# Attention with block sums and a gated FFN on one core: the transpose of the block sums ahead of a unit's stores, their copies a step later, and one pair's neighbor keys three steps sooner

## The chip, the core and the metric

The kernel runs on one core of a Trainium2 chip. The core has five engines with a queue of instructions each: PE (TensorE, matrix products, with its weight loads shown apart as PEld), DVE (VectorE), ACT (ScalarE), POOL (GpSimd, here almost only the issuer of loads) and SP (SyncE, here only an issuer of stores and of transposing DMAs). Each queue runs in order. The metric is the device time of one execution in microseconds; the median of several runs counts.

## What is computed

Sparse attention for 4 batches, 8 heads, 768 tokens of width 64: every token sees its neighbors at a distance under 16 and, for each of the 24 blocks of 32 tokens, the maximum of the block's keys with the mean of the block's values. Then a gated feed-forward layer with a residual gate over the 3072 tokens.

```python
k_sum = k.reshape(B, H, nb, block, D).max(axis=3)
v_sum = v.reshape(B, H, nb, block, D).mean(axis=3)
scores_l = where(|i - j| < 16, scale * q @ k.T, -1e9)
scores_s = scale * q @ k_sum.T + log(block)
a = softmax(concat([scores_l, scores_s]))
x = a @ concat([v, v_sum])                      # heads side by side: 3072 x 512
ffn = (gelu(x @ w_gate) * (x @ w_val)) @ w_out  # 512 -> 1536 -> 512
out = x + sigmoid(x @ w_res) * ffn
```

## The kernel before

The work is cut into eight units (`u` 0 to 7), each one half of a batch: 384 tokens (`TU`). Batch is `b = u // 2`, `half = u % 2`, and the batch to be prepared next is `nb = b + 1`. The order of the instructions is written out by hand, and each engine runs its queue in that order; semaphores make an instruction wait for what it reads and for what it overwrites.

A unit begins with the twelve steps `fo` 0 to 11 of the FFN's first layer. Each step makes the products `g` and `vv` on PE (L398, four matmuls each), the Gelu `ge` on ACT (L404) and the product `gvT` on DVE (L405). `g` and `vv` lie in four PSUM accumulators (tag `mm`) that are used in turn. Between the steps, small pieces that prepare the next unit or batch are put in: `values_step(u, fo)` and the `if` lines of the loop. After the twelve steps comes the rest of the unit: the scores of the next unit (`s_step`, L330, then the exponential on ACT and the mask on DVE, L347), the residual gate (`res_step`, L416, L422), the second FFN layer (`ffn_step`, L432), the products with the values (`av_step`, L362, scaled on DVE at L370 and L372 into `xn`), the transposes of `xn` (`xt_step` on PE, L381, or `xt_dma` on SP, L386), and per 128 tokens `end_step`, which makes `o` on DVE (L437, L439) and stores it (L443). The stores go by SP's queue in units 0, 1, 2 and 7 and by POOL's in units 3 to 6.

The operands of the attention are prepared like this:

- `kW` (one tile per batch parity and pair of heads, pairs 0 to 3) holds for each 64-token tile its own keys, 16 neighbor keys on each side, and the 24 block maxima; `qT` holds the transposed queries. `turn_batch(b, p0, p1)` transposes keys and queries of pairs p0 to p1-1 from `k_sb` and `q_sb` by DMA on SP: per pair two for `kW` (L251) and one for `qT` (L254). For batch 1, pairs 2 and 3 are turned at the start of unit 1, pairs 0 and 1 by PE.
- `k_rest(kw)` then makes the block maxima (L209, L211) and copies the neighbor keys (L213, L214) and the maxima (L215). For batch 1 all of it is on DVE; for batches 2 and 3 the two neighbor copies are on ACT.
- `vext` holds the values; `v_spread` (L291, L294) copies them on DVE to the odd tiles. For batches 2 and 3 the block sums come in four pieces: `turn_values` transposes the values on SP (L261, in step 0 of units 2 and 4), `block_sums` sums them on DVE into `vsT` (L267, steps 8 to 11 of units 2 and 4), `turn_sums` transposes `vsT` into `vsB` by one DMA on SP (L271), and `vsum_bc` copies `vsB` into rows 96 to 127 of `vext` (L303), on ACT for the first half of the batch in units 3 and 5, on DVE for the second half in units 4 and 6.

In the kernel before, `turn_sums` is issued in step 0 of units 3 and 5, so on SP's queue it stands behind what the unit before it issued there. The three lines that matter for its place:

```python
if half == 1 and 1 < nb < B and fo == 0:
    turn_sums()
    turn_batch(nb, NP - 1, NP)
```

Of the kernel before, what the change touches and what calls it, by code (L numbers as in the profile page):

```python
# [15 lines left out]
def kernel(  # L16
# [11 lines left out]
    nc = tc.nc  # L28
    B, H, S, D = q.shape
# [8 lines left out]
    FO = DFF // 128  # L38
    QT = 64
    NT = S // QT  # L40
    HT = NT // 2
# [3 lines left out]
    NP = H // 2  # L45
# [27 lines left out]
    kW = [[const.tile([128, NT, 128], BF16, name=f"kW{i}_{p}") for p in range(NP)] for i in range(2)]  # L73
# [30 lines left out]
    with tc.manual_schedule():  # L104

        def vext_consts(i):
            nc.vector.memset(vext[i][:, :, :, D:D + 1], 1.0)
            nc.vector.memset(vext[i][0:WIN, 0], 0.0)
            nc.vector.memset(vext[i][64:96, NT - 1], 0.0)
            nc.vector.memset(vext[i][64:64 + WIN, NT - 1, :, D:D + 1], 1.0)  # L110
# [57 lines left out]
        def gate(t):  # L168
            nc.gpsimd.tensor_copy(tick[:], t)
# [36 lines left out]
        def k_rest(kw, copy=nc.vector.tensor_copy):  # L206
            own = kw[:, :, OWN:OWN + QT].rearrange("d t (n w) -> d t n w", w=BLK)
            km = work.tile([128, NT, 2, BLK // 2], BF16, tag="km", name="km")
            nc.vector.tensor_max(km[:], own[:, :, :, 0:BLK // 2], own[:, :, :, BLK // 2:BLK])  # L209
            ks = work.tile([128, NB], BF16, tag="ks", name="ks")  # L210
            nc.vector.tensor_reduce(out=ks.rearrange("d (t n) -> d t n", n=2), in_=km[:],  # L211
                                    axis=mybir.AxisListType.X, op=ALU.max)
            copy(kw[:, 1:NT, 0:WIN], kw[:, 0:NT - 1, OWN + QT - WIN:OWN + QT])  # L213
            copy(kw[:, 0:NT - 1, POST:POST + WIN], kw[:, 1:NT, OWN:OWN + WIN])  # L214
            nc.vector.tensor_copy(kw[:, :, BLK0:BLK0 + NB], ks.unsqueeze(1).to_broadcast([128, NT, NB]))  # L215
# [30 lines left out]
        def turn_batch(b, p0, p1):  # L246

            for hp in range(p0, p1):
                kt = kW[b % 2][hp].rearrange("d (c e) m -> d c e m", e=2)
                for e in range(2):  # L250
                    nc.sync.dma_start_transpose(  # L251
                        out=kt[:, :, e, OWN:OWN + QT],
                        in_=k_sb[b][64 * e:64 * e + 64, hp].rearrange("p c d -> p (c d)"))
                nc.sync.dma_start_transpose(  # L254
                    out=qT[b % 2][hp].rearrange("d (c m) -> d c m", c=NC),
                    in_=q_sb[b][:, hp].rearrange("p c d -> p (c d)"))
# [8 lines left out]
        def block_sums(vT, hp):  # L265
            with nc.allow_low_precision("block means are bf16 operands"):
                nc.vector.tensor_reduce(out=vsT[:, hp, 96:96 + NB], in_=vT[:, hp].rearrange("d (n w) -> d n w", w=BLK),  # L267
                                        axis=mybir.AxisListType.X, op=ALU.add)

        def turn_sums():  # L270
            nc.sync.dma_start_transpose(out=vsB[:], in_=vsT.rearrange("d p n -> d (p n)"))  # L271
# [15 lines left out]
        def v_spread(b, c0, c1, part):  # L287

            V = vext[b % 2].rearrange("p (c e) h d -> p c e h d", e=2)
            if part == 0:  # L290
                nc.vector.tensor_copy(V[0:64, c0:c1, 1, :, 0:D], V[64:128, c0:c1, 0, :, 0:D])  # L291
            else:
                hi = min(c1, NC - 1)
                nc.vector.tensor_copy(V[64:96, c0:hi, 1, :, 0:D], V[0:32, c0 + 1:hi + 1, 0, :, 0:D])  # L294

        def vsum_bc(b, hp, lo, hi, mul=nc.vector.tensor_scalar_mul):
            dst = vext[b % 2][96:128, lo:hi, 2 * hp:2 * hp + 2, 0:D]
            if b < 2:
                src = vsum[b][96:128, 2 * hp:2 * hp + 2, 0:D]
                nc.vector.tensor_copy(dst, src.unsqueeze(1).to_broadcast([32, hi - lo, 2, D]))  # L300
            else:
                src = vsB[96:128, hp].rearrange("p (h d) -> p h d", d=D)
                mul(dst, src.unsqueeze(1).to_broadcast([32, hi - lo, 2, D]), 1.0 / BLK)  # L303
# [89 lines left out]
        def half_fo(st, w, fo, lo, hi, acc=None):  # L393
            fs = slice(fo * 128, (fo + 1) * 128)
            if acc is None:
                acc = ps_mm.tile([128, 512], F32, tag="mm", name="g" if w is w_gate else "vv")
            for ko in range(lo, hi):
                nc.tensor.matmul(acc[:, 0:TU], w[:, ko, fs], st["xT"][:, ko, :],  # L398
                                 start=(ko == 0), stop=(ko == KO - 1))
            return acc  # L400

        def fo_end(gvT, fo, g, vv):
            ge = work.tile([128, TU], F32, tag="ge", name="ge")
            nc.scalar.activation(ge[:], g[:, 0:TU], AF.Gelu)  # L404
            nc.vector.tensor_mul(gvT[:, fo, :], ge[:], vv[:, 0:TU])  # L405

        def fo_step(st, gvT, fo):
            g = half_fo(st, w_gate, fo, 0, KO)
            vv = half_fo(st, w_val, fo, 0, KO)
            fo_end(gvT, fo, g, vv)  # L410
# [40 lines left out]
        def values_step(u, fo):  # L451

            b = u // 2 + 1
            if u in (2, 4) and fo >= FO - NP:
                block_sums(vT[b], fo - FO + NP)
            if u in (3, 5):
                if fo in (1, 3):
                    v_spread(b, 0, HT // 2, fo // 2)
                if 5 <= fo < 9:
                    vsum_bc(b, fo - 5, 0, HT, nc.scalar.mul)  # L460
            if u % 2 == 0 and u < NU - 1:
                if fo in (0, 1):
                    v_spread(b - 1, HT // 2, NC, fo)
                if 2 <= fo < 2 + NP:
                    vsum_bc(b - 1, fo - 2, HT, NT)
# [66 lines left out]
        for u in range(NU):  # L532
            b, half = u // 2, u % 2
            nb = b + 1
# [15 lines left out]
            for fo in range(FO):  # L550
                if u == 0 and fo < 2:
                    for w, _, acc in firsts[2 * fo:2 * fo + 2]:
                        half_fo(st, w, fo, KO - 1, KO, acc)
                    fo_end(gvT, fo, firsts[2 * fo][2], firsts[2 * fo + 1][2])
                elif u > 3 and fo == 0:
                    fo_end(gvT, fo, firsts[0][2], firsts[1][2])
                elif u > 3 and fo == 1:
                    fo_end(gvT, fo, firsts[2][2], half_fo(st, w_val, fo, 0, KO))
                else:
                    fo_step(st, gvT, fo)  # L560
                values_step(u, fo)
                if u == 0 and fo == 4:
                    nc.vector.memset(vsT[:], 0.0)
                    load_rows(1)
                if u == 0 and fo == 6:
                    vext_consts(1)
                if u == 0 and fo == FO - 1:
                    kw_consts(1)
                    for c in range(NC + 1):
                        load_values(1, c)  # L570
                if u == 2 and fo == FO - 1:
                    gate(gvT[0:1, fo, 0:1])
                    load_rows(3)
                if half == 0 and 1 < nb < B and fo == 0:
                    vT[nb] = turn_values(nb)
                    turn_batch(nb, 0, NP - 1)
                if half == 1 and 1 < nb < B and fo == 0:
                    turn_sums()
                    turn_batch(nb, NP - 1, NP)
                if half == 1 and 1 < nb < B and fo in (0, 2, 4, 11):  # L580
                    k_rest(kW[nb % 2][(0, 2, 4, 11).index(fo)], nc.scalar.copy)
                if u == 1 and fo == 6:
                    gate(gvT[0:1, fo, 0:1])
                    load_batch(2)
                if u == 1 and fo in (1, 2, 6, 7):
                    home = TT if fo % 2 else AO
                    if fo < 4:
                        k_step(nb, fo - 1, *home)
                    else:
                        q_step(q_sb[nb], nb, 0, S, fo - 6, *home)  # L590
                if u == 1 and fo == FO - 1:
                    k_rest(kW[1][2])
                    k_rest(kW[1][3])
                if u == 0 and fo >= FO - 4:
                    k_later(kW[0][fo - FO + 4])
                if u == 0 and fo in (FO - 3, FO - 2):
                    for hp in range(2 * (fo - FO + 3), 2 * (fo - FO + 3) + 2):
                        q_step(qb, 0, TU, S, hp, *(TT if hp % 2 else AO))
# [120 lines left out]
```

The softmax here doesn't subtract the row's maximum and nothing guards it: scores larger than these inputs give would overflow.

## Time and profile before

| | |
|---|---|
| median of 5 runs | 260.9 us (260.07 to 261.66) |
| the profiled execution | 261.14 us, span 259.2 us |
| granted TensorE clock | 1.00 |
| PE busy | 249.5 us, 96% |
| DVE busy | 173.8 us, 67% |
| ACT busy | 140.1 us, 54% |
| POOL busy | 101.1 us, 39% |

The span runs from the first to the last instruction in the profile; the execution's own time holds what lies around it too. Times of rows count from the span's start. A row of a timeline gives start, duration, engine, line, operation, what it writes and reads, and in brackets how long the engine had been idle before it and what ended that. A row of waits gives who waited for whom, the total, how often, and the longest. A row of DMA issues ends with the time from issue to landing. In the chain that ended last, each piece is followed by what it released.

### The profile page before, as it was taken

Reading aid. Unit: us, or ns where it says so; the run is one execution under the profiler, and the core shown is the slowest. Engines: PE = TensorE matmul, PEld = TensorE weight load, DVE = VectorE, ACT = ScalarE, POOL = GpSimd, SP = SyncE. Lnnn points to the kernel's source line nnn. Section 1 sums busy time; section 2 is a strip of 40 time slices with the busy share of each in tenths; the row PEclk is TensorE's granted clock in tenths of the full one; section 3 lists DMA queues with packets and bytes.
Section 4 is the critical chain, followed back from the end, with each engine's and each line's share of the span. In section 5 each row is a group of like instructions: output and inputs, shape, how many; then the busy total and the mean of one; then the engine's idle time right before and its main releaser. Section 6 shows DMA issues by size and latency. Waiting matters only on the chain.

```text
span 259.2 us, 5743 instructions
## 1 busy us (share of the span) xinstructions
PE 249.5 (96%) x2223; PEld 140.0 (54%) x2249; DVE 173.8 (67%) x402; ACT 140.1 (54%) x247; POOL 101.1 (39%) x139
## 2 busy tenths in 40 slices
PE   7989999999999999999799999999999999999994
PEld 3545655566535565556455565456654565556543
DVE  4665975496498869669457778579658754674424
ACT  3574359544655636665784436647783537353310
POOL 7995543793889901997630100020000100020000
PEclk9999999999999999999999999999999999999999
DMA  7999999999999999999991975456003200130012
GB/s 154 153 155 190 197 204 197 143 198 138 149 149 166 174 149 153 133 180 205 152 118 30 169 154 91 48 144 91 0 3 87 83 0 1 33 137 3 0 40 81
DMA packets 117898, 30.15 MB, mean 116 GB/s; under 512 B 104816, under 2 KB 115504, under 8 KB 117872
## 3 DMA queue, kind: packets, MB, share of 16 engines
q0 software_dynamic: 86640, 19.11, 84.5%
q1 hardware_dynamic: 31232, 10.69, 23.8%
q8 instruction: 17, 0.28, 0.5%
q14 instruction: 9, 0.07, 0.1%
HBM read 32.51 MB, written 6.29 MB: 150 GB/s over the span
## 4 chain that ended last, share of the span: by engine, by line
PE 86%; DVE 7%; issue 3%; ACT 2%; DMA 1%; DVEq 0%; ACTq 0%
PE f L432 22%; PE vv L398 21%; PE g L398 20%; PE r L416 8%; PE ao L362 3%; PE gv L548 3%; PE s L330 2%; PE xp L381 1%; DMA kf<-in_k_dram 1%; DVE ks L211 1%; PE s L449 1%; PE tp L226 1%; DVE gvT L405 1%; DVE vext L300 1%; DVE th L437 1%
## 5 line engine op out<-in xcount | busy, mean ns | idle before, releaser
L398 PE MATMUL vv<-xT,w_val 128*128 128x384 bf16 x364 | 74.5, 326 | 1.7 <-ACT ge L404 1.7
L405 DVE TENSOR_TENSOR gvT<-ge,vv 128x384 bf16<-128x384 f32 x91 | 49.7, 551 | 32.4 <-PE vv L398 25.4
L398 PE MATMUL g<-xT,w_gate 128*128 128x384 bf16 x348 | 71.3, 326 | 0.0
L404 ACT ACTIVATE ge<-g 128x384 f32<-128x384 f32 x87 | 42.7, 491 | 52.0 <-DVE gvT L405 26.7
L432 PE MATMUL f<-w_out,gvT 128*128 128x512 bf16 (+2 forms) x298 | 66.5, 362 | 0.8 <-issue 0.2
L398 PEld LDWEIGHTS <-w_val 128*128 128x128 bf16 x368 | 36.0, 98 | 25.6 <-issue 2.0
L398 PEld LDWEIGHTS <-w_gate 128*128 128x128 bf16 x352 | 34.1, 98 | 22.2
L432 PEld LDWEIGHTS <-gvT 128*128 128x128 bf16 x312 | 28.3, 98 | 28.2
L443 POOL DMA_DIRECT2D out_dram<-o x12 | 6.6, 546 | 93.6 <-DVE rz L370 78.7
L422 ACT ACTIVATE th<-r 128x512 f32<-128x512 f32 x24 | 14.2, 602 | 23.6 <-PE r L416 23.6
L437 DVE SCALAR_TENSOR_TENSOR th<-th,f 128x512 f32<-128x512 f32 (+2 forms) x26 | 16.7, 642 | 12.3 <-PE f L432 8.5
L416 PE MATMUL r<-w_res,xT 128*128 128x512 bf16 x88 | 24.0, 380 | 0.4
L100 POOL DMA_DIRECT2D vext<-in_v_dram x28 | 23.2, 863 | 2.1 <-DMA v_sb<-in_v_dram 2.0
L175 POOL DMA_DIRECT2D k_sb<-in_k_dram x24 | 19.8, 844 | 10.4 <-DMA w_out<-in_moe_w_out_dram 5.2
L347 DVE TENSOR_TENSOR P<-P,maskt 128x768 bf16<-128x768 bf16 x28 | 15.4, 557 | 9.5 <-ACT P L339 5.3
L175 POOL DMA_DIRECT2D q_sb<-in_q_dram x24 | 19.8, 872 | 1.1 <-DMA k_sb<-in_k_dram 0.9
L372 DVE TENSOR_TENSOR xn<-ao,rz 128x384 bf16<-128x384 f32 x32 | 17.8, 558 | 1.1
L383 ACT COPY xT<-xp 128x384 bf16<-128x384 bf16 x20 | 9.3, 482 | 16.5 <-PE xp L381 16.5
L439 DVE SCALAR_TENSOR_TENSOR o<-th,xn 128x512 f32<-128x512 f32 (+2 forms) x26 | 16.9, 651 | 0.9
L336 ACT ACTIVATE P<-s,bias_t 128x384 bf16<-128x384 f32 x32 | 16.8, 579 | 1.1 <-PE s L330 1.1
L339 ACT ACTIVATE P<-s,bias_t 128x768 bf16<-128x768 f32 x16 | 14.5, 904 | 4.3 <-PE s L330 4.3
L175 POOL DMA_DIRECT2D v_sb<-in_v_dram x16 | 13.2, 871 | 1.8 <-DMA q_sb<-in_q_dram 1.8
(102 smaller groups left out, 242.0 us busy)
## 6 DMA issues: line engine op xcount, KB each, us to landing
out_dram<-o POOLq DMA_DIRECT2D x12, 256.0 KB, 2.3
out_dram<-o SPq DMA_DIRECT2D x11, 256.0 KB, 4.4
vext<-in_v_dram POOLq DMA_DIRECT2D x20, 128.0 KB, 7.0
k_sb<-in_k_dram POOLq DMA_DIRECT2D x24, 96.0 KB, 7.0
q_sb<-in_q_dram POOLq DMA_DIRECT2D x24, 96.0 KB, 5.3
w_gate<-in_moe_w_gate_dram POOLq DMA_DIRECT2D x6, 256.0 KB, 9.5
w_val<-in_moe_w_val_dram POOLq DMA_DIRECT2D x6, 256.0 KB, 10.0
w_out<-in_moe_w_out_dram POOLq DMA_DIRECT2D x3, 512.0 KB, 14.1
```

The lines of the kernel that those rows point to most:

```text
L100: nc.gpsimd.dma_start(out=dst, in_=v[b, :, lo:hi, :].rearrange("h p d -> p h d"))
L175: nc.gpsimd.dma_start(out=sb[b][:, h // 2, :, h % 2 * D:h % 2 * D + D], in_=src[b, h].rearrange("(c p) d -> p c d", c=NC))
L336: nc.scalar.activation(P[:, hh].rearrange("p t q -> p (t q)"), s[hh][:, 0:TU], AF.Exp, scale=scale, bias=bias_t[:])
L347: nc.vector.tensor_mul(Pf, Pf, maskt.unsqueeze(1).to_broadcast([128, 2 * HT, QT]))
L372: nc.vector.tensor_mul(xn, ao[:, :, :, 0:D], rz.to_broadcast([128, NSUB, 2, D]))
L398: nc.tensor.matmul(acc[:, 0:TU], w[:, ko, fs], st["xT"][:, ko, :], start=(ko == 0), stop=(ko == KO - 1))
L404: nc.scalar.activation(ge[:], g[:, 0:TU], AF.Gelu)
L405: nc.vector.tensor_mul(gvT[:, fo, :], ge[:], vv[:, 0:TU])
L416: nc.tensor.matmul(r[:], st["xT"][:, ko, ss], w_res[:, ko, :], start=(ko == 0), stop=(ko == KO - 1))
L432: nc.tensor.matmul(st["f", sub][:, 0:c1 - c0], gvT[:, fo, ss], w_out[:, fo, c0:c1], start=(fo == 0), stop=(fo == FO - 1))
L437: nc.vector.scalar_tensor_tensor(th, th, 1.0, f[:, 0:c1 - c0], ALU.add, ALU.mult)
L439: nc.vector.scalar_tensor_tensor(o[:, 0:c1 - c0].rearrange("p (k d) -> p k d", d=128), th.rearrange("p (k d) -> p k d", d=128), 0.5, st["x ...
```

## The change

Three things move; nothing is added or removed. First, `turn_sums` is issued in step 11 of units 2 and 4 instead of step 0 of units 3 and 5: on SP's queue it then stands ahead of unit 2's stores, and in unit 4 ahead of the three `xt_dma`. `turn_batch` of pair 3 stays in step 0. Second, the four `vsum_bc` on ACT in units 3 and 5 go from steps 5 to 8 to steps 6 to 9. Third, in unit 1 the `k_rest` of pair 2 of batch 1 goes from step 11 to step 8; that of pair 3 stays in step 11.

```diff
             if u in (3, 5):
                 if fo in (1, 3):
                     v_spread(b, 0, HT // 2, fo // 2)
-                if 5 <= fo < 9:
-                    vsum_bc(b, fo - 5, 0, HT, nc.scalar.mul)
+                if 6 <= fo < 10:
+                    vsum_bc(b, fo - 6, 0, HT, nc.scalar.mul)
...
                 if half == 1 and 1 < nb < B and fo == 0:
+                    turn_batch(nb, NP - 1, NP)
+                if half == 0 and 1 < nb < B and fo == FO - 1:
                     turn_sums()
-                    turn_batch(nb, NP - 1, NP)
...
-                if u == 1 and fo == FO - 1:
-                    k_rest(kW[1][2])
-                    k_rest(kW[1][3])
+                if u == 1 and fo in (8, FO - 1):
+                    k_rest(kW[1][2 if fo == 8 else 3])
```

## The prediction

> **What bounds the kernel now.** I read the page's engine row and the chain that ended last first.
>
> ```profile
> PE 249.5 (96%) x2223; PEld 140.0 (54%) x2249; DVE 173.8 (67%) x402; ACT 140.1 (54%) x247; POOL 101.1 (39%) x139
> ...
> PE 86%; DVE 7%; issue 3%; ACT 2%; DMA 1%; DVEq 0%; ACTq 0%
> ```
>
> TensorE sets the time; only the 14% of the chain that is not PE can be won. The chain of waits in order of time puts the long stretches off PE, after the start, at 70 to 80 us (unit 1's end) and 116 to 126 us (unit 3's first steps). The first PE products of units 2 to 7 come at 85.44, 114.31, 144.57, 172.94, 201.30 and 229.67: units 4, 5 and 6 take 28.4 us each, unit 3 takes 30.26. So unit 3 loses 1.9.
>
> The waits of PE, then the timelines of SP, ACT, DVE and PE around that place, and (line with 8.0) the issue of the block sums' transpose with its time to landing:
>
> ```profile
> PE vv L398 <- ACT ge L404: 1.7, 1, 1.7
> ...
> 108.06 1.39 SPq L254 DMA_TRANSPOSE qT<-q_sb  x1
> 109.59 6.60 SPq L443 DMA_DIRECT2D out_dram<-o  x3
> 116.24 1.97 SPq L271 DMA_TRANSPOSE vsB<-vsT  x1
> ...
> vsB<-vsT SPq DMA_TRANSPOSE x1, 8.0
> ...
> 124.39 0.85 ACT L303 ACTIVATE vext<-vsB 32x768 bf16<-32x768 bf16 x1 [2.40 <-DMA v_sb<-in_v_dram]
> 125.26 0.49 ACT L404 ACTIVATE ge<-g 128x384 f32<-128x384 f32 x1
> ...
> 124.23 0.55 DVE L405 TENSOR_TENSOR gvT<-ge,vv 128x384 bf16<-128x384 f32 x1
> ...
> 123.24 0.81 PE L398 MATMUL g<-xT,w_gate 128*128 128x384 bf16 x4
> 125.80 0.81 PE L398 MATMUL vv<-xT,w_val 128*128 128x384 bf16 x4 [1.74 <-ACT ge L404]
> ```
>
> To be seen: the transpose of the sums stands in SP's queue behind unit 2's three stores, the last of which waits for its `o` until 115.83. It is issued at 116.24 and lands at 116.24 + 8.0 = 124.24. ACT's first row copy, program step 5 of unit 3, starts 0.15 after that, so vsB released it, not the v_sb load that the row names. The Gelu of step 6 is queued behind it on ACT, and PE's `vv` of step 7 starts 0.04 after that Gelu ends at 125.76.
>
> For unit 1 I read the DVE chain, the PE weight loads and the SP issue of pair 2:
>
> ```profile
> 70.53 0.36 DVE km L209
> ...
> 77.13 1.87 DVE vext L300 x4
> ...
> 79.27 0.57 DVE xn L372
> 79.88 0.34 PE xp L381 x3
> ...
> 77.80 0.68 PEld L362 LDWEIGHTS <-P 128*64 128x64 bf16 x24 [0.42 <-DVE vext L300]
> 79.88 0.17 PEld L381 LDWEIGHTS <-xn 128*128 128x128 bf16 x3 [0.57 <-DVE xn L372]
> ...
> 57.27 1.69 SPq L251 DMA_TRANSPOSE kW<-k_sb  x1
> ...
> kW<-k_sb SPq DMA_TRANSPOSE x1, 9.2
> ...
> 66.16 0.56 DVE L405 TENSOR_TENSOR gvT<-ge,vv 128x384 bf16<-128x384 f32 x1 [1.08 <-PE vv L398]
> ```
>
> From 70.06 to 79.84 DVE runs without a pause, with two `k_rest` at its head (70.53 to 72.97), and PE waits for its products.
>
> **Part 1, the sums' transpose ahead of the stores (unit 3).** The sums are ready at 102.64 (last reduce 101.69 + 0.95), but SP is still issuing pairs 0 to 2 until 108.06 + 1.39 = 109.45, so the transpose goes out near 109.5 without a wait. It holds SP 1.2 to 2.0 us, its own two rows in this trace. Behind it the first store slips from 109.59 to about 111; nobody waits for that store. The second waits for its `o` until 113.92 anyway, so the queue has caught up, and pair 3's two kW and one qT transposes start at 116.3 instead of 118.3. Landing takes 2.5 to 8.0 (both rows of this transpose): 112.0 to 117.5. Wanted, after the move to step 6: g of step 6 ends at 122.75, its Gelu at 123.3. The margin is 5.8 us, so I take the wait as gone.
>
> Removed: `vv` of step 7 would start at 123.24 + 0.65 = 123.89 and starts at 125.80: **1.91 us**.
>
> What is late next is DVE. In steps 0 to 4 it does five `gvT`, three `k_rest` and two spreads without a gap from 116.28, and ends the gvT of step 5 at 124.78. PE's four accumulators serve two products a step. That `vv` 7 follows Gelu 6 by 0.04 means that it takes the accumulator of g 6; then each g takes that of the `vv` three steps back. g of step 8 would be due at 123.24 + 1.30 = 124.54 and must wait for 124.78 + 0.04: **0.28 us comes back**. Bounds: 0, if the accumulators fall otherwise; and if each product took the one freed two steps back, `vv` 7, due 123.89, would wait until 124.82: 0.94. I take 0.28, the order that the `vv` 7 row shows. So unit 3 gives 1.63, between 0.97 and 1.91.
>
> The Trainium skill speaks against this part: its page "DMA: Bandwidth & Descriptors", section on the anatomy of one DMA, fits about 2 us plus bytes over 436 GB/s for a transfer (it is measured on the GpSimd path); for 128x512 bf16 an estimate of 2.3 us. By that the old issue at 116.24 would have landed at 118.5, no copy would have waited, and the move would be worth nothing. The row's 8.0 us decides.
>
> **Part 2, row copies one step later (units 3 and 5).** Same four copies, 0.85 each. With a Gelu they make a step of 1.38 on ACT (125.26 to 126.64) against PE's 1.30, so the Gelu after the fourth is 4 x 0.08 = 0.32 late. With the accumulators as above, `vv` of a step needs the Gelu before it, which normally ends 0.6 ahead (g lasts 0.81, Gelu 0.49 and hand-overs 0.05 after a start 1.95 before the `vv`). Cost nothing, as in unit 5 now, where the same four copies at 180.64 to 185.65 stop no product; if that cover were gone, 0.32 a unit. Step 11's own ACT copies follow one free step later.
>
> **Part 3, the sums' transpose in unit 4.** Its stores go by POOL, and SP's queue is busy with qT of pair 2 until 162.2, past the last reduce at 161.77; then SP idles until the first xT at 166.34. The 1.2 us transpose fits there; xT is not delayed. In unit 5 pair 3's transposes come 1.3 sooner; no copy waited there before. Worth nothing either way.
>
> **Part 4, `k_rest` of pair 2 at step 8 (unit 1).** One `k_rest` lasts 70.53 to 71.75, 1.22 us, and leaves the chain of 70 to 80. PE's gaps there, from starts against its own rate: `ao` of pair 0 at 77.80 where f ends its six at 77.70 (0.10), 24 `ao` in 0.73 where unit 2's take 0.50 (0.23), `xp` at 79.88 where three f end at 79.64 (0.24): 0.57. Unit by unit: unit 1 is 32.42; unit 2's 28.87, four turns of 0.33 and 1.73 for the means give 31.92, so 0.50 is lost. With DVE 1.22 sooner, the vsum copy on ACT (75.64 + 0.58) is late next: the four vext copies run 76.26 to 78.13, in time for both `ao`, and xn ends before 79.3. I take **0.50**, bounds 0 and 0.57.
>
> Its new place is step 8, after the gvT at 66.16. Pair 2's second transpose lands at 57.27 + 9.2 = 66.47, or 66.62 with the 0.15 seen above; `k_rest` would begin at 66.63. That is a tie. Behind a wait there stand the gvT of steps 9 to 11. DVE idles 0.74 before each now, 2.22 in all, against 1.22 of work: a landing up to 1.0 later costs nothing in the chain, and up to 1.8 still leaves it no later than before. The copies could also be slower beside POOL's issues (0.67 and 0.63 at 57.8 and 57.9 against 0.19 and 0.22 at 71.5 and 71.6), about 0.6 more, inside that margin.
>
> Units 2 on then start 0.5 sooner. Unit 2's vT of pair 1 lands at 89.05 + 9.6 = 98.65, its reduce would be asked at 98.47 instead of 99.04: 0.3 of waiting on DVE, whose gaps there are 0.74 a step; no cost.
>
> **Sum.** 1.63 + 0.50 = 2.13. The profiled execution is 261.14 (span 259.2): it would be 259.0. The median of the runs is 260.9, 0.24 under it: **258.8**.
>
> **Rivals.**
> 1. DVE's backlog replaces more of ACT's wait (0.94) and unit 1 gives nothing because DVE waits at step 8: 260.9 - 0.97 = 259.9. For: the tie at 66.6, and DVE busy without a gap from 116.28 to 124.78. Against: the `vv` 7 row. 0.13.
> 2. The move in unit 3 does not do what it says: the sums still land after 123.3. That needs 13.8 us from issue, where this transpose took 8.0; k_sb loads reach 15.3. Then only unit 1's 0.50: 260.4. 0.04.
> 3. Slower: at step 8 DVE stands behind pair 2's landing. Beyond 1.8 us of lateness each further one moves the chain of 70 to 80, and with it PE; it decides from 1.8 + 1.63 + 1.3 = 4.7, a landing 13.9 after issue. At 6 us it is 6 - 1.8 - 1.63 = 2.6 slower: 263.5. Against: these transposes and their neighbours took 7.8 to 9.8. 0.06.
>
> **How the numbers follow.** The forecast has 0.77. Range: the full 1.91 + 0.57 gives 258.4, less 0.4 because five runs spread over 260.07 to 261.66: 258.0; at the top rivals 1 and 2: 260.4. Half a per cent, 1.3 us, is about what a measurement of this kernel can tell from no change. Faster 0.77, within 0.17 (rivals 1 and 2), slower 0.06.
>
> **What would show it.** Right: vsB issued before the three out_dram rows of unit 2, near 109, and no L303 row on ACT with an idle before it; PE's 1.74 at `vv` gone, a wait of `g` for gvT of about 0.3 near step 8; unit 3 of 28.4 to 28.9; `km` at about 66.6 in unit 1 and unit 1 at 31.9. Wrong: a DVE wait at L209 over 2 us, a PE wait near step 11 of unit 1, or unit 3 still above 29.5.

## The result, and the profile after

The changed kernel takes 258.82 us (median of 44 runs, 257.72 to 260.94), the kernel before 260.24 us (79 runs, 258.83 to 263.39). The ratio is 0.9945, with a 95% interval of 0.9931 to 0.9958: faster by 0.55%, 1.4 us. The profiled execution took 258.95 us, its span 257.1 us. The five runs of the kernel before that the prediction started from had a median of 260.9, 0.7 above that of the 79; the forecast of 258.8 met the time by luck in part, since its start was 0.7 too high and its gain 0.7 too large. Of the gain of 2.1 that it forecast, 1.4 came (1.1 to 1.8 by the interval).

From the page of the changed kernel, the engines and the chain that ended last, then the waits of PE:

```profile
PE 248.3 (97%) x2223; PEld 139.3 (54%) x2249; DVE 173.3 (67%) x402; ACT 140.0 (54%) x247; POOL 100.8 (39%) x139
...
PE 83%; DMA 8%; POOL 5%; DVE 1%; issue 1%; POOLq 0%; DVEq 0%
...
PE vv L398 <- DVE gvT L405: 0.6, 1, 0.6
```

Every engine has the same number of instructions as before. The wait of `vv` for the Gelu, 1.7 before, is gone from PE's list, and one of 0.6 for `gvT` has come. The first comes from unit 3, the second from unit 1. Unit 3 in the timelines of SP, ACT and PE, with the issue of the sums' transpose and its time to landing:

```profile
108.75 1.34 SPq L254 DMA_TRANSPOSE qT<-q_sb  x1
110.19 1.33 SPq L271 DMA_TRANSPOSE vsB<-vsT  x1
111.61 4.32 SPq L443 DMA_DIRECT2D out_dram<-o  x3
...
vsB<-vsT SPq DMA_TRANSPOSE x1, 6.9
...
122.54 0.49 ACT L404 ACTIVATE ge<-g 128x384 f32<-128x384 f32 x1 [0.81 <-PE g L398]
123.05 0.85 ACT L303 ACTIVATE vext<-vsB 32x768 bf16<-32x768 bf16 x1
...
123.64 0.81 PE L398 MATMUL vv<-xT,w_val 128*128 128x384 bf16 x4
124.29 0.81 PE L398 MATMUL g<-xT,w_gate 128*128 128x384 bf16 x4
```

The transpose goes out straight behind qT of pair 2 and lands at 110.19 + 6.9 = 117.1. The first row copy, at 123.05, has no idle time before it, and PE keeps its pace of 0.65 a product through the whole unit. Unit 1, DVE and PE, with the issue of pair 2's second key transpose:

```profile
66.97 0.36 DVE L209 TENSOR_TENSOR km<-kW 128x384 bf16<-128x384 bf16 x1 [1.11 <-DMA kW<-k_sb]
71.44 0.36 DVE L209 TENSOR_TENSOR km<-kW 128x384 bf16<-128x384 bf16 x1 [0.92 <-DMA kW<-k_sb]
...
69.04 0.81 PE L398 MATMUL vv<-xT,w_val 128*128 128x384 bf16 x4 [0.59 <-DVE gvT L405]
...
56.38 1.93 SPq L251 DMA_TRANSPOSE kW<-k_sb  x1
...
kW<-k_sb SPq DMA_TRANSPOSE x1, 10.5
```

DVE now waits at both `k_rest`. Pair 2 lands at 56.38 + 10.5 = 66.88, and `km` starts 0.09 later, 1.1 after DVE was free for it. Behind it the `gvT` of steps 9 and 10 are late, and PE's `vv` of step 11 stands 0.59. (The row counts from the end of the product before it; against PE's pace, which would have had it at 68.29, `vv` is 0.75 late.) Pair 3, which nobody waited for before, is waited for 0.92.

The starts of each unit's first product on PE, subtracted, say where the time went; all profiled kernels of this study are in the table. Units 4 to 6 take 28.36 or 28.37 in every one of them. (These are the first rows of the timelines; the starts in the prediction lie about 0.16 later.)

| profiled kernel | unit 1 starts | unit 1 | unit 2 | unit 3 |
|---|---|---|---|---|
| before | 52.85 | 32.43 | 28.86 | 30.27 |
| whole change | 52.00 | 33.02 | 28.87 | 28.36 |
| whole change, again | 51.91 | 33.97 | 28.87 | 28.36 |
| edits 1 and 2 | 52.47 | 32.93 | 28.93 | 28.56 |
| edit 3 alone | 51.97 | 32.67 | 28.87 | 29.61 |
| edit 1 alone | 52.08 | 32.70 | 28.87 | 28.70 |
| edit 1 alone, again | 51.94 | 32.74 | 28.87 | 28.36 |
| edit 2 alone | 52.01 | 32.84 | 29.89 | 28.36 |
| pair 2 in step 10 | 52.37 | 31.94 | 28.87 | 28.37 |
| and pair 3 after the spreads | 51.68 | 33.06 | 28.88 | 28.52 |
| whole change, keys issued first | 52.35 | 32.93 | 28.86 | 28.37 |
| step 10, keys issued first | 52.14 | 31.94 | 28.87 | 28.50 |
| the same without edit 2 | 52.50 | 31.95 | 28.86 | 28.37 |

Between the two profiles unit 3 gives 1.91 and unit 1 takes 0.59. Unit 1 is the same program in five of these kernels, those without edit 3, and took 32.43 to 32.93 there; the profile before has the shortest of the five, so the 0.59 is an upper estimate. The other 0.85 of the spans' difference lies ahead of unit 1, where the two kernels issue the same; the profiled run of the kernel before was 0.9 over its median, so that part is not the change's.

### The profile page after: what moved, and what is told of

Its sections match the earlier page's. It is cut to its first block, busy times and chain, and to the rows that moved or that the text cites. A ratio compares the mean times of both kernels' runs of the same rounds, so it can differ in the third digit from the quotient of the medians.

```text
span 257.1 us, 5742 instructions
## 1 busy us (share of the span) xinstructions
PE 248.3 (97%) x2223; PEld 139.3 (54%) x2249; DVE 173.3 (67%) x402; ACT 140.0 (54%) x247; POOL 100.8 (39%) x139
## 4 chain that ended last, share of the span: by engine, by line
PE 83%; DMA 8%; POOL 5%; DVE 1%; issue 1%; POOLq 0%; DVEq 0%
PE f L432 24%; PE vv L398 21%; PE g L398 20%; PE r L416 8%; DMA w_val<-in_moe_w_val_dram 4%; DMA w_gate<-in_moe_w_gate_dram 3%; PE gv L548 3%; PE ao L362 3%; PE s L330 2%; POOL vext L100 2%; PE xp L381 1%; POOL k L91 1%; POOL qa L91 1%; PE vs L279 1%; POOL w_gate L160 1%
```

## The experiments

Edit 1 is the sums' transpose ahead of the stores, edit 2 the copies a step later, edit 3 the `k_rest` of pair 2 in step 8. Two theories: A, edit 3 does not pay, since pairs 2 and 3 land at times that no edit here moves; B, the prediction's, it is worth 0.5 and the profile above met a late landing. Each ratio below is to runs of the kernel before made beside it; their medians are 260.70 for the first four experiments, 260.25 for the next four, and 260.16 for the last two and the repeat of edit 1 alone.

**Edits 1 and 2.** The kernel before with

```diff
-                if 5 <= fo < 9:
-                    vsum_bc(b, fo - 5, 0, HT, nc.scalar.mul)
+                if 6 <= fo < 10:
+                    vsum_bc(b, fo - 6, 0, HT, nc.scalar.mul)
...
                 if half == 1 and 1 < nb < B and fo == 0:
-                    turn_sums()
                     turn_batch(nb, NP - 1, NP)
+                if half == 0 and 1 < nb < B and fo == FO - 1:
+                    turn_sums()
```

> The first two edits (transpose of the sums ahead of the stores, copies a step later) without the third (k_rest of pair 2 stays in step 11). Theory A, from the changed kernel's profile: the third edit costs, because DVE stands at step 8 behind pair 2's landing and PE then waits 0.6 at step 11; without it unit 3 keeps its 1.9 gain (28.4 us long), unit 1 falls back from 33.0 to about 32.4, and the kernel is 1.9 under the kernel before, ratio about 0.9925, faster than the whole change. Theory B, the prediction's: the third edit is worth 0.5, and the wait in that profile was an unlucky landing; this kernel then gains less than the whole change does, about 1.0 of its 1.4 us, ratio about 0.996.

Measured: 0.9935 (0.9907 to 0.9964), 259.0 us. That is at or under the whole change's 0.9945, as A says, but the intervals overlap. Unit 1 did not come back to 32.4: pair 3's landing is late here too (a DVE wait of 0.41 at 71.87), and PE waits 0.58 at `ao` for the vext copies at the end of the chain behind it. A smaller wait at `ao`, 0.35 and 0.39, stands in the two profiles of edit 1 alone, where neither `km` waits for a landing.

**Edit 3 alone.**

```diff
-                if u == 1 and fo == FO - 1:
-                    k_rest(kW[1][2])
-                    k_rest(kW[1][3])
+                if u == 1 and fo in (8, FO - 1):
+                    k_rest(kW[1][2 if fo == 8 else 3])
```

> The third edit alone (k_rest of pair 2 of batch 1 in step 8 of unit 1). Theory A: DVE waits about 1 us at L209 in step 8, PE 0.3 to 0.6 at vv of step 11, and pair 3's k_rest starts no sooner than its landing near 71 us, so nothing is won at the unit's end: unit 1 is 32.4 to 33.0 long, the kernel unchanged or up to 0.6 slower, ratio 1.000 to 1.002. Theory B: unit 1 is 31.9 long and the kernel 0.5 faster, ratio 0.998. Unit 3 keeps its wait of 1.7 to 1.9 under both.

Measured: 1.0004 (0.9972 to 1.0037), 260.52 us. The interval, from 0.7 us faster to 1.0 slower, shows no worth of edit 3 by itself. DVE waits 1.08 and 0.66 at the two `km`, PE 0.32 at `vv` of step 11. Unit 3 kept a wait, but a smaller one (29.61) than was expected: the sums took 7.4 us to land in this run, not 8.0. The row of the first copy names the sums as what it waited for, as the prediction had inferred:

```profile
123.10 0.85 ACT L303 ACTIVATE vext<-vsB 32x768 bf16<-32x768 bf16 x1 [1.74 <-DMA vsB<-vsT]
```

**Edit 1 alone**, the second half of the first diff, run twice.

> The first edit alone: the transpose of the sums ahead of the stores, with the copies still in steps 5 to 8. Theory A: the sums land near 117 and the copies of step 5 ask for them near 122, so the whole 1.9 of unit 3 goes without the copies' move; ratio about 0.9925. Rival: with the copies in step 5 the Gelus run late just where DVE's backlog is deepest, and 0.3 to 0.9 of the 1.9 comes back as a wait of PE near steps 7 and 8; ratio 0.994 to 0.9965.

> The first edit alone once more, beside the last two. Its first measurement was the best of all, 0.9921; if the third edit is worth nothing as it stands, it comes again at or under the whole change, 0.992 to 0.9945, with unit 3 of 28.4 to 28.7 and unit 1 of 32.4 to 32.9.

Measured: 0.9921 (0.9894 to 0.9949) and, again, 0.9946 (0.9917 to 0.9975). Edit 1 makes the whole gain of the change (0.9945). The rival's return wait is there in the first profile, PE's row first, with a copy of DVE that ran before it and the loads that POOL issued meanwhile:

```profile
124.39 0.81 PE L398 MATMUL g<-xT,w_gate 128*128 128x384 bf16 x4 [0.18 <-DVE gvT L405]
...
120.86 1.01 DVE L294 COPY vext<-vext 32x1536 bf16<-32x1536 bf16 x1
...
120.56 1.74 POOL L175 DMA_DIRECT2D v_sb<-in_v_dram  x2 [1.73 <-DMA q_sb<-in_q_dram]
```

This is `g` of step 8, which the prediction named; it starts 0.34 later than the pace from 123.40 allows. In the second profile it is not there. It goes with how long DVE's copies take: the same copies, L215 and L294, took 0.57 and 1.01 in the first profile and 0.23 and 0.69 in that of the whole change, where the wait was 0. Edit 2 does not prevent it: `g` of step 8 is also 0.20, 0.16 and 0.14 late in three profiles that have both edits (unit 3 of 28.56, 28.52 and 28.50 in the table). In all four a value spread (L291 or L294) of 0.94 to 1.05 stands ahead on DVE; in the other profiles without the Gelu wait the two spreads took 0.69 to 0.94.

**Edit 2 alone**, the first half of the first diff.

> The second edit alone: the copies in steps 6 to 9, the transpose of the sums still behind the stores. The sums land near 124.2; the first copy, wanted at 123.3, still waits about 1 us, and the Gelu of step 7 behind it ends near 125.75, 0.6 after the product that needs it was due. Theory A: PE's wait in unit 3 shrinks from 1.9 to 0.6, a gain of 1.3, ratio 0.995. Rival: the wait only moves a step and stays at 1.5 or more; ratio 0.998 or above.

Measured: 0.9967 (0.9936 to 0.9999), 259.92 us, between the two expectations. In its profile unit 3 is 28.36, so the wait is gone altogether, more than the 1.3 expected, since the transpose landed in 7.1 us instead of 8.0. But unit 2 lost 1.0. The first copy on ACT, and unit 2's last block sum on DVE:

```profile
124.04 0.85 ACT L303 ACTIVATE vext<-vsB 32x768 bf16<-32x768 bf16 x1 [0.16 <-DMA vsB<-vsT]
...
104.69 0.95 DVE L267 TENSOR_REDUCE vsT<-vT 128x24 bf16<-128x768 bf16 x1 [1.96 <-DMA vT<-v_sb]
```

With edit 2 alone the copy meets the landing almost exactly; with edit 1 beside it, it has about 6 us of room (117.1 to 123.05). And the transposed values are a third place where a landing holds DVE and then PE: the chain that ended last goes from the landing of `vT` through this sum and two masks to PE's `ao` at 106.17. Nothing in the edit reaches it.

**The whole change again, and pair 2 in step 10.**

> The whole change as it is, once more, beside the next three on the same chip: ratio near 0.9945 to the kernel before. In its profile, under the theory that landings in unit 1 come at times that PE does not move (pair 2 near 66.9, pair 3 near 71.3): a DVE wait at L209 of about 1 us in step 8, one before pair 3's k_rest, and unit 1 of 32.5 to 33.0 us.

```diff
-                if u == 1 and fo in (8, FO - 1):
-                    k_rest(kW[1][2 if fo == 8 else 3])
+                if u == 1 and fo in (10, FO - 1):
+                    k_rest(kW[1][2 if fo == 10 else 3])
```

> The whole change with the k_rest of pair 2 in step 10 instead of 8; pair 3's stays in step 11. If pair 2's landing is what holds DVE in step 8, that wait is gone here (asked near 68.9, landed near 66.9) and with it PE's 0.3 to 0.6 at step 11: 0.3 to 0.6 under the whole change. If pair 3's landing near 71.3 sets the rest of unit 1 in both, the end of the unit moves by less: 0 to 0.3. If step 8 is harmless, no difference, or slower by the 0.2 that DVE's backlog grows at step 11.

Measured: 0.9947 (0.9918 to 0.9976) and 0.9940 (0.9917 to 0.9963). The times do not tell them apart, the profiles do. The whole change, DVE and PE:

```profile
67.88 0.36 DVE L209 TENSOR_TENSOR km<-kW 128x384 bf16<-128x384 bf16 x1 [2.11 <-DMA kW<-k_sb]
72.39 0.36 DVE L209 TENSOR_TENSOR km<-kW 128x384 bf16<-128x384 bf16 x1 [1.07 <-DMA kW<-k_sb]
...
69.84 0.81 PE L398 MATMUL vv<-xT,w_val 128*128 128x384 bf16 x4 [1.48 <-DVE gvT L405]
```

With pair 2 in step 10, DVE:

```profile
68.75 0.35 DVE L209 TENSOR_TENSOR km<-kW 128x384 bf16<-128x384 bf16 x1
70.70 0.36 DVE L209 TENSOR_TENSOR km<-kW 128x384 bf16<-128x384 bf16 x1 [0.19 <-DMA kW<-k_sb]
```

In step 8 a landing 0.9 later than in the first profile makes PE's wait 0.9 longer, and unit 1, at 33.97, longer than the 33.0 at most that was expected. In step 10 pair 2 is not waited for, pair 3 hardly, and unit 1 is 31.94, the length that the prediction forecast for edit 3.

**Pair 3 later as well.**

```diff
-                if u == 1 and fo in (10, FO - 1):
-                    k_rest(kW[1][2 if fo == 10 else 3])
+                if u == 1 and fo == 10:
+                    k_rest(kW[1][2])
...
                 v_spread(1, 0, HT // 2, 1)
+                k_rest(kW[1][3])
                 end_step(u, st, 0)
```

> As the last one, and the k_rest of pair 3 behind the value spreads after step 11 instead of in step 11, so that DVE asks for pair 3 near 73.5, after its landing. Theory A (the landings of pairs 2 and 3 hold DVE, so that moving pair 2 alone can't shorten unit 1): no wait at L209, DVE's chain 1.2 shorter up to the masks, PE's wait at ao gone or under 0.2, unit 1 about 32.0 to 32.3, and 0.5 to 0.8 under the whole change, ratio about 0.992. Theory C (what holds unit 1 is DVE's amount of work alone): the same work stands before the vext copies, and nothing is won against the last kernel.

Measured: 0.9950 (0.9926 to 0.9973), unit 1 of 33.06: a miss for A. There is no wait at L209, yet PE waits at `ao`, as the timelines of DVE and PE show:

```profile
70.91 0.56 DVE L347 TENSOR_TENSOR P<-P,maskt 128x768 bf16<-128x768 bf16 x1 [1.08 <-ACT P L339]
74.31 0.36 DVE L209 TENSOR_TENSOR km<-kW 128x384 bf16<-128x384 bf16 x1
...
77.40 0.66 PE L362 MATMUL ao<-vext,P 128*64 128x65 bf16 x24 [0.70 <-DVE vext L300]
```

DVE stands idle for 1.08 until the exponential comes, and then has the 1.24 of `k_rest` in the chain that ends in the vext copies. Theory C is right in this: whatever stands between the masks and those copies costs PE. So landing and load both count: a `k_rest` must come after its landing and before the masks.

**Keys issued first.** The whole change, with SP's order in unit 1 changed; `turn_batch` takes a letter that says which transposes it issues.

```diff
-                turn_batch(1, 2, NP)
+                turn_batch(1, 2, NP, "k")
+                turn_batch(1, 2, NP, "q")
```

> The whole change with the four key transposes of pairs 2 and 3 on SP's queue before their two query transposes, instead of keys and queries pair by pair: pair 3's keys are issued near 58.5 instead of 60.3. Theory A: they land about 1.8 sooner, near 69.5, before step 11 asks for them, and the DVE wait before pair 3's k_rest goes; that before pair 2's in step 8 stays, with PE's 0.3 to 0.6 at step 11. Unit 1 is 32.2 to 32.6, 0.3 to 0.6 under the whole change. If the landing follows the load of the DMA engines and not the order of issue, pair 3 lands as late as before, and nothing changes.

Measured: 0.9964 (0.9935 to 0.9992), unit 1 of 32.93. DVE, then PE (the lines of this kernel are one higher behind `turn_batch`):

```profile
67.81 0.36 DVE L209 TENSOR_TENSOR km<-kW 128x384 bf16<-128x384 bf16 x1 [1.59 <-DMA kW<-k_sb]
71.02 0.35 DVE L209 TENSOR_TENSOR km<-kW 128x384 bf16<-128x384 bf16 x1
...
69.62 0.81 PE L399 MATMUL vv<-xT,w_val 128*128 128x384 bf16 x4 [0.82 <-DVE gvT L406]
```

Pair 3's wait is gone, as A said, and no wait at `ao` is left. But unit 1 is longer than the 32.2 to 32.6 expected, and the median, 259.18, is not under the 258.94 of the whole change beside it. What remains of unit 1's loss, 32.93 against 31.94, is the wait behind step 8 alone: `vv` at 69.62 instead of 68.64.

**Step 10 with the keys issued first**, and the same without edit 2.

> The whole change with the k_rest of pair 2 in step 10 and, on SP's queue, the key transposes of both pairs ahead of their queries. If late landings are all that keeps the third edit from paying, neither pair is waited for here (pair 2 asked near 68.8, landed 66.5 to 67.9; pair 3 asked near 70.5, landed 69.5 to 70.9): unit 1 of 31.9 to 32.1 us, 1.0 shorter than with step 8, ratio 0.990 to 0.993. If the landing times still decide, a wait at L209 stays and unit 1 is over 32.4.

> As the last one, without the second edit: the copies of the sums stay in steps 5 to 8. The order alone took most of unit 3's wait (28.70 against 28.36 us), so this should be 0 to 0.35 slower than the last one, by PE's wait for gvT at step 8 alone; ratio 0.990 to 0.9945. If the copies' move matters more than that, unit 3 is over 28.9.

Measured: 0.9916 (0.9886 to 0.9945), 258.01 us, and 0.9927 (0.9900 to 0.9954), 258.40 us. Unit 1 is 31.94 and 31.95. DVE of the first:

```profile
68.52 0.35 DVE L209 TENSOR_TENSOR km<-kW 128x384 bf16<-128x384 bf16 x1
70.20 0.35 DVE L209 TENSOR_TENSOR km<-kW 128x384 bf16<-128x384 bf16 x1
```

Neither pair is waited for. Step 10 with the keys first is the best median of the study, 0.8 under the whole change's; the two intervals overlap, so the profiles carry that verdict more than the times. Against edit 1 alone, run beside it, the times are clearer: 258.01 against 258.97, and the slowest of its 12 runs, 258.71, is under the other's median. Edit 2 on top of edit 1 can't be told from nothing.

The starts on PE split unit 1's loss in two. Where nothing waits, `vv` of step 11 starts 16.29 after the unit's first product, and the rest of the unit takes 15.66. The five kernels without edit 3 lose nothing up to that `vv`, and 0.47 to 0.98 behind it. With pair 2 in step 8 and the queue's order as it was, only 0.24 to 0.37 is lost behind it, but 0.48 to 1.65 up to it. With pair 2 in step 10 and pair 3 in step 11 both are 0. So edit 3 did win about half a microsecond at the unit's end, and the wait that it made at step 8 took it back.

## Why the prediction was right, and where not

- **Unit 3's wait, 1.91 removed: right.** Cause, place and size held: the sums' transpose behind the stores, and 30.27 - 28.36 = 1.91 between the profiles. Edit 1 alone shows that the order did it. The wait varies between executions, one for one with the landing. The first row copy started 10.25 after the unit's first product before (124.39 - 114.14) and 9.59 after it with edit 3 alone (123.10 - 113.51), 0.66 apart; PE lost 1.91 and 1.25 (29.61 - 28.36), also 0.66 apart. How much of it the runs without a profile had is not shown.
- **0.28 back through DVE: right in place, too large here.** 0 in the changed kernel's two profiles, 0.14 to 0.34 at `g` of step 8 in four others, each time 0.05 to 0.06 after the end of the `gvT` of step 5, the one that the prediction named. The bound of 0.94 was not reached.
- **Edit 2 at nothing: right** beside edit 1. Its ACT steps are 1.39, and no product waits for them.
- **Edit 1 in unit 4 at nothing: right.** Unit 4 is 28.37 before and after, unit 5 28.36.
- **Edit 3, 0.50 gained: wrong, and this is the term that failed.** Instead of -0.50, unit 1 changed by +0.59 and, in the second profile, +1.54 against the profile before; the times of edit 3 alone show no change. Three parts of that step fell. The tie at 66.6 was taken at the one landing seen (9.2 us); the same transpose then took 10.5 and 11.4, and `km` waited until 66.9 to 67.9. The unit also began 0.9 sooner in these profiles, while the landing did not; the twelve profiles that have it put it between 66.4 and 68.4. The margin of 1.0 was counted for DVE's chain alone: PE's `vv` of step 11 waits for the `gvT` of step 9. DVE's waits of 1.08, 1.11, 1.59 and 2.11 in step 8 went with waits of PE of 0.32, 0.59, 0.82 and 1.48, so a wait of DVE costs PE from 0.5 to 0.8 on. And pair 3 was not looked at. It landed at 62.23 + 7.8 = 70.0 before, 1.7 ahead of its `km`; step 11 would now ask for it at 70.5, a margin of 0.5. The rows before:

```profile
62.23 1.41 SPq L251 DMA_TRANSPOSE kW<-k_sb  x1
...
kW<-k_sb SPq DMA_TRANSPOSE x1, 7.8
...
71.75 0.35 DVE L209 TENSOR_TENSOR km<-kW 128x384 bf16<-128x384 bf16 x1
```

The mechanism behind the 0.50 was real: the prediction worked out 31.92 for a unit 1 without loss, and 31.94 is reached where neither landing holds PE.

- **Rivals.** Rival 3, DVE behind pair 2's landing, is what happened in part, with waits of DVE of 1.1 to 2.1 us and not the 4.7 from which it would have decided.
- **The signs.** Unit 3 showed the signs of being right, the 0.3 at `g` apart. Unit 1 showed signs of being wrong: a wait of PE at step 11 in both profiles of the whole change (0.59 and 1.48), and in the second a wait of DVE at L209 over 2 us (2.11).

With the 0.50 left out, the prediction's own sum is 1.63, against 1.4 measured (1.1 to 1.8).

## What to carry to other kernels

A transpose that waits in a queue for a store it has nothing to do with is cheap to find: compare the time its operands were ready with its time of issue, and put it ahead. A step that reads a DMA's result may be moved forward only by the distance to the landing, and one landing is no measure of that: look at several, and at every later DMA that the moved work was hiding. When a tie shows, move less far: here one step instead of three gave unit 1 the length that step 8 was meant to give.

## What the runs showed of the hardware

The transpose of the sums landed in 6.4 to 8.2 us in unit 3, where the DMA engines are 90% busy or more by the pages' slices. It landed in 3.2 to 3.7 us when issued near 160, where the slices fall from 50 to 80% down to 20 to 50%, and in 2.5 us near 171, in a slice of 50%. The key transposes of unit 1 took 7.8 to 11.4. The estimate of 2.3 us from the Trainium skill, "DMA: Bandwidth & Descriptors", section on the anatomy of one DMA, where its fit is for the GpSimd path, agrees with the rows of 2.5 only.

The copies on DVE varied between executions: the neighbor copy L213 took from 0.20 to 0.65, a value spread L294 of 32x1536 from 0.69 to 1.07. The 13 profiles, taken together from 50 to 240 us, say when. Of the copies of L213, L214, L215, L291, L294 and L300, 185 overlapped no DMA issue of POOL, and each of them took the short time of its form: 0.19 to 0.20 for L213 and L214, 0.69 to 0.70 for the spread L294 named above. Every longer one was among the 335 that overlapped such an issue, as in the rows of edit 1 alone. DVE's reductions and its instructions with two operands kept their times within 0.07 either way. The Trainium skill, "SBUF — State Buffer", section "Who interferes with whom", names a port that DVE and GpSimd hold in turn, which would fit POOL's loads at those times; no run here takes the loads away, so the cause is not shown.
